# Attention, expert routing and MLP on one core: a build-time estimate that also counts DMA queues, and another order of the first list's vector steps

## The chip, the cores and the metric

The kernel runs on one core of a Trainium2 chip. Its time is the device time of one execution in microseconds (us). Engines are named as the profile names them: PE is TensorE (PEld its weight load), DVE VectorE, ACT ScalarE, POOL GpSimd, SP SyncE, which here only issues transfers.

## The reference, cut to what matters

```python
def reference(**kwargs):
    attn_out = _attn_ref(q, k, v)                    # (2, 8, 768, 64): local window plus block summaries
    x = attn_out.transpose(0, 2, 1, 3).reshape(1536, 512)
    x = _moe_ref(x, w_gate, w1, w2)
    return _moe2_ref(x, w_in, w_out)

def _moe_ref(x, w_gate, w1, w2):                     # 8 experts, 192 tokens each
    logits = x @ w_gate
    for idx in np.argsort(-logits.flatten()):        # greedy: best pair first, until each expert is full
        tok, e = idx // 8, idx % 8
        if assigned[tok] < 0 and counts[e] < 192:
            assigned[tok] = e; counts[e] += 1
    for e in range(8):
        mask = assigned == e
        out[mask] = np.maximum(x[mask] @ w1[e], 0) @ w2[e]

def _moe2_ref(x, w_in, w_out):                       # 512 -> 2048 -> 512
    r = np.maximum(x @ w_in, 0)
    return (r * r) @ w_out
```

## The kernel before, in words

The program has three stretches. Up to about 95 us attention runs, with its projections onto the expert logits. Up to about 318 us routing and experts run side by side: routing finds, one expert after the other, the list of the 192 tokens of the expert that fills up next, and an expert whose list is there is computed while the next lists are found. Then comes the last MLP, `_moe2_ref`, in 48 steps.

**Routing** (function `routing`). For each list DVE compares keys (L566), PE counts (L578), and from the counts come the expert and its threshold. Then DVE picks the tokens, PE sums over them (L786, L787), DVE scans (L790) and turns the positions into two small one-hot arrays (function `t_hot`, L846 to L852). PE multiplies these (`t_idx`, L860), DVE spreads the product (`t_spread`, L869), PE sums (`t_sum`, L878), and POOL gathers the rows of x by the indices (`t_gather`, L904 and L906), into `xa` and `xb`. Between the scan and `t_hot` stand four DVE steps that belong to the next list: `ua` (L802), `cap` (L796), the update of the logits (L797) and `kt` (L820). For the first list they stand behind `t_hot`, for the others ahead of it.

**Experts** (functions `x_t`, `expert`). `x_t` transposes the gathered rows on PE (the row transposes, L942 and L944). An expert has 32 matmuls with w1 (L961) into four tiles, which ACT brings into `ht` (L966), and 32 with w2 (L978) into two tiles, which ACT and DVE split into `yhi` (L984) and `ylo` (L985). The weights of an expert are four tiles, loaded by SP (`w_load`, L931, two transfers of 512 KB each).

**Conversions** (function `conv_stream`). The last MLP multiplies in a form that needs each fp32 weight as a high and a low part. The 4 MB of w_in and 4 MB of w_out are cut into 32 pieces of 512 KB, eight for each quarter of the hidden units. Piece i is loaded by SP into a buffer `raw` (L621), of which there are two. DVE then makes four steps: the first (L636) and second (L640) on piece i, the low part of piece i-1 (L643), and the third step on piece i (L646); ACT makes the high part (L639). The third step is the last reader of the buffer, so piece i+2 can only be loaded behind the third step of piece i:

```python
            nc.vector.scalar_tensor_tensor(fi, raw[:, :, 1], -0x40000000, fi, op0=OP.bitwise_and, op1=OP.bitwise_or)
            nfree[0] = i + 3
            if not eager[0] and i + 2 < len(todo):
                conv_load(i + 2)
```

**What sets the order.** Each engine runs its instructions in the order in which the program was written, and that order is made when the program is built. The class `Clock` (variable `T`) keeps an estimated time for PE, DVE, ACT and POOL; each piece of code adds its estimated cost. The main loop of `moe` takes, whenever the estimated PE is free, the next piece of routing, of row transposes or of an expert, whichever the estimate says can start first. `t_gather` notes when the gathered rows are thought to be there (`d["tx"]`), and `conv_idle` puts conversion steps where the estimate has DVE idle, if the piece is thought to be loaded (`landed`):

```python
        while nload[0] < min(nfree[0], len(todo)) and freed[nload[0]] <= T.pe:
            landed[nload[0]] = T.pe + 5.0
            conv_load(nload[0])
```

**The last MLP.** Step i multiplies by w_in (`hmm`, L1070, 12 matmuls), ACT applies ReLU (L1073), DVE squares (L1074), ACT makes the high part (L1078), DVE the low part (L1079). The square and the low part of one step are called a pair below. Two steps later the result is multiplied by w_out (`omm`, L1096, 12 matmuls). Between two pairs stand six conversion steps in the first 12 steps, until all 32 pieces are converted, with more where a quarter's weights have to be complete (ahead of steps 4, 8 and 12).

Of the kernel before, what the change touches and what calls it, by code (L numbers as in the profile page):

```python
# [9 lines left out]
F32 = mybir.dt.float32  # L10
# [6 lines left out]
OP = mybir.AluOpType  # L17
# [4 lines left out]
N, DM, E, F, FF = 1536, 512, 8, 1024, 2048  # L22
CAP = N // E
NB = S // 32
NBLK = N // 128
# [389 lines left out]
BIG = 2.0 ** 120  # L415
# [4 lines left out]
class Clock:  # L420


    def __init__(self):
        self.pe = self.dve = self.act = self.pool = 0.0

    def p(self, us, after=0.0):
        self.pe = max(self.pe, after) + us
# [164 lines left out]
def moe(tc, nc, R0, x_dram, m_dram, L9, w1, w2, win, wout, out, identf, identb, dbg=None):  # L592
# [19 lines left out]
    nload, nfree, eager = [0], [2], [True]  # L612
# [51 lines left out]
    rp = R0.rp  # L664
    sctx = ExitStack()
    p_s = sctx.enter_context(tc.tile_pool(name="m_ps", bufs=1, space=PSUM, reuse_waits="tile"))
    wt9, low, ones, dead, zero24 = R0.wt9, R0.low, R0.ones, R0.dead, R0.zero24
# [5 lines left out]
    T = Clock()  # L673
# [11 lines left out]
    def routing():  # L685
        tm_at = T.v(0.1)
        for ph in range(E):
            d = st[ph] = {}
            ei = rp.tile([128, 8], U32, name="ei", bufs=4)
            es = rp.tile([128, 1], F32, name="es")  # L690
# [14 lines left out]
            m, mw, o, no = R0.m, R0.mw, R0.o, R0.no  # L705
# [38 lines left out]
            if ph < E - 1:  # L744
                tm = R0.tm
                yield tm_at + 0.1
                ps = p_s.tile([128, 128], F32, name="ms", bufs=3)
# [7 lines left out]
                th = m8[:, 0:1]  # L755
                nc.vector.tensor_scalar(es, ei[:, 0:1], -1.0, 15.0, op0=OP.mult, op1=OP.add)
                T.v(0.9, T.pe + 0.25)
            else:
# [5 lines left out]
                ps = p_s.tile([128, 128], F32, name="ms", bufs=3)  # L764
# [20 lines left out]
            ps = p_s.tile([128, 48], F32, name="ms", bufs=3)  # L785
# [2 lines left out]
            T.p(0.07, sel_at + 0.1)  # L788
            sc = rp.tile([128, 24], F32, name="sc")
            nc.vector.tensor_tensor_scan(sc, ps[:, 24:48], zero24, 0.0, op0=OP.add, op1=OP.add)  # L790
            a = rp.tile([128, NBLK], F32, name="ua")
            cap = rp.tile([128, E], F32, name="cap")

            def full():
                if ph < E - 1:
                    nc.vector.tensor_scalar(cap, wt9[:, 0, 0:E], es, -2 * BIG, op0=OP.is_equal, op1=OP.mult)  # L796
                    nc.vector.tensor_tensor(L9[:, :, 0:E], L9[:, :, 0:E],  # L797
                                            cap[:, None, :].to_broadcast([128, NBLK, E]), op=OP.add)

            def over_th():  # L800
                if ph < E - 1:
                    nc.vector.tensor_scalar(a, m, th, None, op0=OP.is_gt)  # L802

            first = ph == 0
            if not first:
                over_th()
            nc.vector.tensor_tensor(sc, ps[:, 0:24], sc, op=OP.add)
            nc.vector.scalar_tensor_tensor(sc, sc, 1.0, s2, op0=OP.add, op1=OP.mult)
            if not first:
                full()  # L810
            s = d["s"] = rp.tile([128, NBLK], I32, name="s")
            nc.vector.tensor_tensor(s, sc[:, 0:NBLK], sc[:, NBLK:], op=OP.add)
            now = ph < 2 or ph >= E - 2
            if first:
                t_hot(ph)
                over_th()
                full()
            if ph < E - 1:
                kt = rp.tile([128, NBLK], F32, name="kt")
                nc.vector.scalar_tensor_tensor(kt, sc[:, NBLK:], CAP + 0.5, sel[:, 1], op0=OP.is_lt, op1=OP.mult)  # L820
            T.v(1.1, T.pe + 0.2)
            if now and not first:
                t_hot(ph)
            if ph < E - 1:
                nc.vector.tensor_tensor(a, a, kt, op=OP.max)
# [73 lines left out]
    def t_gather(ph):  # L899

        d = st[ph]
        xa = d["xa"] = f1.tile([128, DM], F32, name="xa")
        xb = d["xb"] = f1.tile([128, DM], F32, name="xb")[0:64, :]
        nc.gpsimd.indirect_dma_start(out=xa, out_offset=None, in_=x_dram,  # L904
                                     in_offset=bass.IndirectOffsetOnAxis(ap=sci[:, d["ka"]:d["ka"] + 1], axis=0))
        nc.gpsimd.indirect_dma_start(out=xb, out_offset=None, in_=x_dram,  # L906
                                     in_offset=bass.IndirectOffsetOnAxis(ap=d["ib"][:, :1], axis=0))
        fl = d["fl"] = rp.tile([1, 1], I32, name="fl", bufs=4)
        nc.gpsimd.memset(fl, 0)
        d["tx"] = T.g(2.3, max(d["ix_at"], T.pe) + 0.1) + 2.8  # L910
        w_next()

    wl, done, used = [(ph, i) for ph in range(E) for i in range(4)], [-1], [8]
# [6 lines left out]
    def w_load(ph, i):  # L920

        d = st[ph]
        eng = nc.sync
        if i == 1:
            eng.value_load(d["fl"][0:1, 0:1], min_val=0, max_val=N - 1)
        r = eng.value_load(d["ei"][0:1, 0:1], min_val=0, max_val=E - 1)
        s1 = w1[bass.ds(r, 1)].rearrange("o (k p) f -> p (o k) f", p=128)
        s2 = w2[bass.ds(r, 1)].rearrange("o (k p) f -> p (o k) f", p=128)
        t = wp.tile([128, 4, 512], F32, name="w8")
        for k in (0, 2):  # L930
            eng.dma_start(t[:, k:k + 2, :], s1[:, k:k + 2, 512 * i:512 * i + 512] if i < 2 else  # L931
                          s2[:, 4 * i - 8 + k:4 * i - 6 + k, :])
        d.setdefault("w", []).append(t)

    def x_t(ph):

# [59 lines left out]
    freed, landed = {}, {}  # L996

    def conv_idle():

        while nload[0] < min(nfree[0], len(todo)) and freed[nload[0]] <= T.pe:  # L1000
            landed[nload[0]] = T.pe + 5.0
            conv_load(nload[0])
        while (R is None or len(st) >= done[0] + 4) and T.dve < T.pe - 0.3 and landed.get(nfree[0] - 2, 1e9) <= T.pe:
            n0, f0 = nstep[0], nfree[0]
            conv_step()
            if nstep[0] == n0:
                return
            T.v(0.7, T.pe - 0.7)
            if nfree[0] > f0:
                freed[nfree[0] - 1] = T.dve + 1.0  # L1010
# [162 lines left out]
```

## Time and profile before

| | us |
|---|---|
| three runs | 584.87, 585.63, 586.07 (median 585.63) |
| the profiled execution, its own time | 588.34 |
| its span in the profile | 586.1 |
| PE busy | 566.9 (97%) |
| DVE busy | 344.7 (59%) |
| ACT busy | 196.5 (34%) |
| POOL busy | 82.4 (14%) |
| granted PE clock, mean | 0.997 |

The profiled execution is 2.24 us longer than its span and 2.71 us longer than the median. A busy share is a mean over three stretches with different limits: in the last MLP alone DVE is busy about 85% of the time as long as conversions run, and under 30% afterwards.

### The profile page before, as it was taken

What the parts mean: (1) busy time and instruction counts of PE and PEld (TensorE: products, weight loads), DVE (VectorE), ACT (ScalarE), POOL (GpSimd) and SP (SyncE); (2) the same over time, 40 slices, a digit from 0 to 9 for tenths busy, and PEclk for the clock granted to TensorE, in tenths of its full rate; (3) what the DMA queues carried; (4) which work ended last, traced back from release to release, by engine and by line L of the source; (5) the groups of instructions that cost most, each with busy time, mean ns of one, the idle gap of its engine ahead of it and who ended that gap; (6) DMA issues with size and microseconds to landing.
All of it is one profiled execution on the core that took longest, in us unless ns stands there. A gap on an engine that the chain in (4) does not pass through costs nothing.

```text
span 586.1 us, 10517 instructions
## 1 busy us (share of the span) xinstructions
PE 566.9 (97%) x4128; PEld 474.9 (81%) x4128; DVE 344.7 (59%) x773; ACT 196.5 (34%) x421; POOL 82.4 (14%) x136
## 2 busy tenths in 40 slices
PE   6999997999999999999899999999999999999996
PEld 4777873698888978999899888878888888888884
DVE  6875788877878879655464888872322222222222
ACT  4877861331322314122122333342222122222221
POOL 7663300110401222010000000000300000300002
PEclk9999999999999999999899999999999999999999
DMA  9997114635285374688542354420100000100001
GB/s 228 264 181 161 65 74 144 241 127 193 97 287 172 144 233 155 243 285 308 215 143 74 110 174 126 130 72 2 72 1 1 1 0 1 72 1 0 1 0 72
DMA packets 55392, 71.33 MB, mean 122 GB/s; under 512 B 21296, under 2 KB 32560, under 8 KB 55344
## 3 DMA queue, kind: packets, MB, share of 16 engines
q1 hardware_dynamic: 53360, 64.38, 35.4%
q0 software_dynamic: 1984, 6.29, 3.1%
q8 instruction: 32, 0.52, 0.4%
q14 instruction: 16, 0.13, 0.1%
HBM read 64.37 MB, written 6.29 MB: 121 GB/s over the span
## 4 chain that ended last, share of the span: by engine, by line
PE 61%; issue 15%; DVE 12%; DMA 7%; ACT 2%; POOL 2%; SPq 0%; POOLq 0%; DVEq 0%; ACTq 0%
PE ph L961 12%; PE ph L978 12%; PE pg L1070 9%; PE ph L1096 7%; PE px L1096 2%; PE O L284 2%; PE cnt L578 2%; DMA raw<-in_moe_w_out_dram 2%; DVE f L646 2%; PE S L250 2%; PE T L270 2%; DVE f L640 2%; DMA raw<-in_moe_w_in_dram 2%; DVE G L566 2%; PE T L193 2%
## 5 line engine op out<-in xcount | busy, mean ns | idle before, releaser
L978 PE MATMUL ph<-ht,w 128*128 128x192 f32 x512 | 91.4, 334 | 2.6 <-ACT ht L966 2.6
L961 PE MATMUL ph<-xt,w 128*128 128x192 f32 x512 | 90.9, 331 | 0.0
L566 DVE TENSOR_SCALAR G<-mrow,m 128x1536 bf16<-128x1536 f32 (+4 forms) x108 | 85.0, 839 | 8.1 <-PE cnt L578 5.2
L978 PEld LDWEIGHTS ph<-ht,w 128*128 128x128 f32 x512 | 84.4, 193 | 6.3 <-ACT ht L966 3.2
L961 PEld LDWEIGHTS ph<-xt,w 128*128 128x128 f32 x512 | 82.5, 190 | 3.2 <-issue 2.3
L1070 PE MATMUL pg<-yhi,w 128*128 128x512 f32 x192 | 59.1, 389 | 0.0
L1074 DVE TENSOR_TENSOR xa<-xa 128x512 f32<-128x512 f32 x24 | 16.6, 691 | 56.3 <-ACT xa L1073 56.3
L1109 POOL DMA_INDIRECT out_dram<-f,sci x6 | 5.9, 979 | 308.2 <-DVE f L1107 307.5
L1074 DVE TENSOR_TENSOR xb<-xb 128x512 f32<-128x512 f32 x24 | 16.6, 692 | 53.6 <-ACT xb L1073 53.3
L1070 PEld LDWEIGHTS pg<-yhi,w 128*128 128x128 f32 x192 | 36.0, 188 | 7.5
L1070 PE MATMUL pg<-ylo,w 128*128 128x512 f32 x96 | 37.3, 389 | 0.0
L1096 PE MATMUL ph<-w,xt 128*128 128x512 f32 x144 | 35.7, 391 | 0.2 <-DVE xt L1079 0.2
L966 ACT ACTIVATE ht<-ph 128x384 f32<-128x384 f32 x32 | 15.7, 490 | 55.2 <-PE ph L961 52.9
L1073 ACT ACTIVATE xa<-pg 128x512 f32<-128x512 f32 x24 | 14.3, 594 | 57.9 <-PE pg L1070 57.9
L1073 ACT ACTIVATE xb<-pg 128x512 f32<-128x512 f32 x24 | 14.3, 594 | 54.6 <-PE pg L1070 54.6
L1096 PEld LDWEIGHTS ph<-w,xt 128*128 128x128 f32 x144 | 26.9, 188 | 6.3 <-DVE xt L1079 0.5
L1070 PE MATMUL pg<-yhi,w2a 128*128 128x512 f32 x96 | 29.7, 391 | 0.0
L1070 PE MATMUL pg<-yhi,w2b 128*128 128x512 f32 x96 | 29.5, 389 | 0.0
L263 ACT ACTIVATE P<-S,nm 128x120 f32<-128x120 f32 x96 | 26.6, 371 | 1.8 <-DVE nm L259 1.8
L984 ACT ACTIVATE yhi<-ph 128x384 fp32r<-128x384 f32 x16 | 7.8, 490 | 56.9 <-PE ph L978 56.9
L636 DVE TENSOR_SCALAR f<-raw 128x512 int32<-128x512 int32 x32 | 13.7, 427 | 19.2 <-DMA raw<-in_moe_w_in_dram 12.3
L904 POOL DMA_INDIRECT xa<-x_dram,sci x8 | 13.4, 1669 | 69.2 <-DVE sci L892 43.5
(242 smaller groups left out, 985.6 us busy)
## 6 DMA issues: line engine op xcount, KB each, us to landing
w<-in_moe_w_dram SPq DMA_DIRECT2D x64, 512.0 KB, 6.2
raw<-in_moe_w_in_dram SPq DMA_DIRECT2D x16, 512.0 KB, 3.8
raw<-in_moe_w_out_dram SPq DMA_DIRECT2D x16, 512.0 KB, 3.3
vw<-in_v_dram SPq DMA_DIRECT2D x16, 240.0 KB, 6.3
rawk<-in_k_dram SPq DMA_DIRECT2D x8, 384.0 KB, 6.4
rawq<-in_q_dram SPq DMA_DIRECT2D x8, 384.0 KB, 6.0
x_dram<-x SPq DMA_DIRECT2D x10, 256.0 KB, 2.3
vw<-in_v_dram SPq DMA_DIRECT2D x8, 80.0 KB, 4.9
```

The costliest lines, as they stand in the source:

```text
L193: nc.tensor.transpose(pr[:, r, :], ROWS[nm, b, hp][:, 3 * half + r, :], identf)
L263: nc.scalar.activation(P[u][:, hh, i], SS[u][hh][:, i], AF.Exp, bias=NM[u][:, hh, i:i + 1])
L566: self.nc.vector.tensor_scalar(t[:, used:used + w], self.mrow[:, 128 * j0:128 * j1], self.m[:, c:c + 1], CS, op0=OP.is_le, op1=OP.mult)
L636: nc.vector.tensor_scalar(fi, raw[:, :, 1], 3, 0x3FFFFFF8, op0=OP.logical_shift_left, op1=OP.bitwise_and)
L904: nc.gpsimd.indirect_dma_start(out=xa, out_offset=None, in_=x_dram, in_offset=bass.IndirectOffsetOnAxis(ap=sci[:, d["ka"]:d["ka"] + 1], ax ...
L961: nc.tensor.matmul(ps[:, j, 0:CAP], w[:, k, 128 * (f % 4):128 * (f % 4) + 128], d["xt"][:, k, :], start=(k == 0), stop=(k == 3), skip_grou ...
L966: nc.scalar.activation(d["ht"][:, f0:f0 + 2, :], ps[:, :, 0:CAP], AF.Relu)
L978: nc.tensor.matmul(ps[:, j, 0:CAP], w[:, f % 4, 128 * dd:128 * dd + 128], d["ht"][:, f, :], start=(f == 0), stop=(f == 7), skip_group_chec ...
L1070: nc.tensor.matmul(ps, a[:, k, fs], b[:, k, js], start=(n == 0), stop=(n == 11))
L1073: nc.scalar.activation(r, ps, AF.Relu)
L1074: nc.vector.tensor_tensor(r, r, r, op=OP.mult)
L1096: nc.tensor.matmul(PO[j][t], a[:, 128 * t:128 * t + 128], b[:, f % 4, :], start=(f == 0 and n == 0), stop=(f == 15 and n == 2))
```

## The change

`Clock` gets a fifth time, for the DMA queues (method `d`). Each weight tile adds 3.1 us to it, each gather 1.0 us, each conversion load 1.6 us. The gathered rows are taken to be there between 0.2 and 1.7 us later than before, by how far the DMA time is ahead. A loaded piece is taken to be there 4.4 us behind the later of PE and DMA time, where it was 5.0 us behind PE. In `routing` the first list gets the order of the other lists. No instruction's operands change, and no piece of work is added or removed but three filler matmuls (35 where there were 32).

```diff
     def __init__(self):
-        self.pe = self.dve = self.act = self.pool = 0.0
+        self.pe = self.dve = self.act = self.pool = self.dma = 0.0
+
+    def d(self, us, after=0.0):
+        self.dma = max(self.dma, after) + us
+        return self.dma
...
-            a = rp.tile([128, NBLK], F32, name="ua")
-            cap = rp.tile([128, E], F32, name="cap")
-
-            def full():
-                if ph < E - 1:
-                    nc.vector.tensor_scalar(cap, wt9[:, 0, 0:E], es, -2 * BIG, op0=OP.is_equal, op1=OP.mult)
-                    nc.vector.tensor_tensor(L9[:, :, 0:E], L9[:, :, 0:E],
-                                            cap[:, None, :].to_broadcast([128, NBLK, E]), op=OP.add)
...
-            first = ph == 0
-            if not first:
-                over_th()
+            if ph < E - 1:
+                a = rp.tile([128, NBLK], F32, name="ua")
+                nc.vector.tensor_scalar(a, m, th, None, op0=OP.is_gt)
             nc.vector.tensor_tensor(sc, ps[:, 0:24], sc, op=OP.add)
+            if ph < E - 1:
+
+                cap = rp.tile([128, E], F32, name="cap")
+                nc.vector.tensor_scalar(cap, wt9[:, 0, 0:E], es, -2 * BIG, op0=OP.is_equal, op1=OP.mult)
             nc.vector.scalar_tensor_tensor(sc, sc, 1.0, s2, op0=OP.add, op1=OP.mult)
-            if not first:
-                full()
+            if ph < E - 1:
+                nc.vector.tensor_tensor(L9[:, :, 0:E], L9[:, :, 0:E], cap[:, None, :].to_broadcast([128, NBLK, E]),
+                                        op=OP.add)
...
-            now = ph < 2 or ph >= E - 2
-            if first:
-                t_hot(ph)
-                over_th()
-                full()
...
-            if now and not first:
+            now = ph < 2 or ph >= E - 2
+            if now:
                 t_hot(ph)
...
-        d["tx"] = T.g(2.3, max(d["ix_at"], T.pe) + 0.1) + 2.8
+        out = T.g(2.3, max(d["ix_at"], T.pe) + 0.1)
+        d["tx"] = out + 3.0 + 0.5 * min(max(T.dma - out, 0.0), 3.0)
+        T.d(1.0, out)
...
         d.setdefault("w", []).append(t)
+        T.d(3.1, T.pe)
...
-            landed[nload[0]] = T.pe + 5.0
+            landed[nload[0]] = T.d(1.6, T.pe) + 2.8
             conv_load(nload[0])
```

Lines move with it. In the order after the change L621 is L625, the DVE steps L636, L640, L643, L646 are L640, L644, L647, L650, ACT's L639 is L643, L966 is L961, L984 is L979, L948 is L943, L931 is L925, L1074 is L1069 and L1079 is L1074.

**ACT, the seventh expert (number 6).** From its row transposes (`xt`) to its second `yhi`; the rows with `f` as input are the conversions' high parts. Before:

```order
L948 ACTIVATE xt<-px 128x2x192
L948 ACTIVATE xt<-ms 128x2x192
L639 ACTIVATE w2a<-f 128x512
L966 ACTIVATE ht<-ph 128x384 x2
L639 ACTIVATE w2a<-f 128x512
L966 ACTIVATE ht<-ph 128x384
L639 ACTIVATE w2a<-f 128x512
L966 ACTIVATE ht<-ph 128x384
L639 ACTIVATE w2a<-f 128x512
L984 ACTIVATE yhi<-ph 128x2x192
L639 ACTIVATE w2a<-f 128x512
```

After the change:

```order
L943 ACTIVATE xt<-px 128x2x192
L943 ACTIVATE xt<-ms 128x2x192
L643 ACTIVATE w2a<-f 128x512
L961 ACTIVATE ht<-ph 128x384 x3
L643 ACTIVATE w2a<-f 128x512
L961 ACTIVATE ht<-ph 128x384
L643 ACTIVATE w2a<-f 128x512
L979 ACTIVATE yhi<-ph 128x2x192
L643 ACTIVATE w2a<-f 128x512
```

(The two rows ahead of these are the row transposes of the last expert, number 7.) Ahead of the expert's fourth `ht` there stood the high parts of pieces 3, 4 and 5; now there stand those of pieces 2 and 3.

**DVE, the last MLP from the second pair to the third.** Rows with `raw` alone as input are first steps, those with `raw,f` second (L640 before, L644 after) and third steps (L646 before, L650 after), those with `f,w2b` low parts. Before:

```order
L1074 TENSOR_TENSOR xa<-xa 128x512
L1079 TENSOR_TENSOR xt<-xa,xt 128x512
L636 TENSOR_SCALAR f<-raw 128x512
L640 SCALAR_TENSOR_TENSOR f<-raw,f 128x512
L643 TENSOR_TENSOR w2b<-f,w2b 128x512
L646 SCALAR_TENSOR_TENSOR f<-raw,f 128x512
L636 TENSOR_SCALAR f<-raw 128x512
L640 SCALAR_TENSOR_TENSOR f<-raw,f 128x512
L1074 TENSOR_TENSOR xb<-xb 128x512
```

After the change:

```order
L1069 TENSOR_TENSOR xa<-xa 128x512
L1074 TENSOR_TENSOR xt<-xa,xt 128x512
L650 SCALAR_TENSOR_TENSOR f<-raw,f 128x512
L640 TENSOR_SCALAR f<-raw 128x512
L644 SCALAR_TENSOR_TENSOR f<-raw,f 128x512
L647 TENSOR_TENSOR w2b<-f,w2b 128x512
L650 SCALAR_TENSOR_TENSOR f<-raw,f 128x512
L640 TENSOR_SCALAR f<-raw 128x512
L1069 TENSOR_TENSOR xb<-xb 128x512
```

The pairs now fall at other places in the round of four conversion steps: this one ahead of a third step, the next behind a first step, where before they fell behind a third and behind a second step. Of the conversion steps, 53 stood ahead of the first pair, and 48 do now.

**SP, from the load of piece 2 on.** The `w_` rows are the second weight tile of expert 7, in two halves. Before:

```order
L621 DMA raw<-in_moe_w_in_dram 128x1024
L925 TENSOR_LOAD fl
L925 ISA x2
L926 TENSOR_LOAD ei
L926 ISA x2
L931 ISA
L931 DMA w_4110<-in_moe_w_dram 128x2x512
L931 ISA
L931 DMA w_4110<-in_moe_w_dram 128x2x512
L621 DMA raw<-in_moe_w_in_dram 128x1024
L621 DMA raw<-in_moe_w_out_dram 128x1024
```

After the change:

```order
L625 DMA raw<-in_moe_w_in_dram 128x1024 x2
L919 TENSOR_LOAD fl
L919 ISA x2
L920 TENSOR_LOAD ei
L920 ISA x2
L925 ISA
L925 DMA w_4114<-in_moe_w_dram 128x2x512
L925 ISA
L925 DMA w_4114<-in_moe_w_dram 128x2x512
```

Piece 3 now stands ahead of this tile. The third and fourth tile of expert 7 follow in both orders; piece 4 stood ahead of them and now stands behind them.

## Rows read from the trace of the kernel before

**Rows 1.** Waits of PE from 95 us on: us in total, times, longest us.
```profile
PE ph L978 <- ACT ht L966: 2.6, 1, 2.6
PE px L942 <- DMA xa<-x_dram,sci: 1.2, 1, 1.2
PE px L944 <- DMA xb<-x_dram,ib: 0.9, 1, 0.9
```

**Rows 2.** Timeline near 287 us, DVE, ACT, PE: start, us, instruction, [idle before <- releaser].
```profile
272.79 0.43 DVE L636 TENSOR_SCALAR f<-raw 128x512 int32<-128x512 int32 x1 [0.97 <-DMA raw<-in_moe_w_in_dram]
...
283.60 0.43 DVE L636 TENSOR_SCALAR f<-raw 128x512 int32<-128x512 int32 x1 [5.72 <-DMA raw<-in_moe_w_out_dram]
...
286.00 0.63 ACT L639 ACTIVATE w2a<-f 128x512 fp32r<-128x512 f32 x1 [5.58 <-DVE f L646]
...
287.06 10.40 PE L978 MATMUL ph<-ht,w 128*128 128x192 f32 x52 [2.62 <-ACT ht L966]
```

**Rows 3.** Chain that ended last, the next 64 matmul records: start us, us, what.
```profile
297.46 10.40 PE ph L961 x64
```

**Rows 4.** Stretch by engine: PE, PEld, DVE, ACT, POOL busy, granted PE clock, DMA.
```profile
290.00:292.00 2.00, 2.00 (x8) 2.00 (x8) 0.96 (x2) 0.00 (x0) 0.00 (x0) 0.52 0.42 168
```

**Rows 5.** Timeline of DVE, last MLP: the second pair to the third, and pair 12.
```profile
327.14 0.68 DVE L1074 TENSOR_TENSOR xa<-xa 128x512 f32<-128x512 f32 x1
328.52 0.69 DVE L1079 TENSOR_TENSOR xt<-xa,xt 128x512 fp32r<-128x512 f32 x1 [0.70 <-ACT xt L1078]
329.13 0.42 DVE L636 TENSOR_SCALAR f<-raw 128x512 int32<-128x512 int32 x1
...
330.80 0.68 DVE L646 SCALAR_TENSOR_TENSOR f<-raw,f 128x512 int32<-128x512 int32 x1
331.40 0.42 DVE L636 TENSOR_SCALAR f<-raw 128x512 int32<-128x512 int32 x1
331.85 0.69 DVE L640 SCALAR_TENSOR_TENSOR f<-raw,f 128x512 int32<-128x512 int32 x1
332.67 0.69 DVE L1074 TENSOR_TENSOR xb<-xb 128x512 f32<-128x512 f32 x1
...
391.52 0.69 DVE L1079 TENSOR_TENSOR xt<-xb,xt 128x512 fp32r<-128x512 f32 x1 [0.70 <-ACT xt L1078]
```

**Rows 6.** Timeline of PE at the w_out matmuls of step 12.
```profile
391.56 0.48 PE L1096 MATMUL ph<-w,xt 128*128 128x512 f32 x1
392.27 2.14 PE L1096 MATMUL ph<-w,xt 128*128 128x512 f32 x8 [0.23 <-DVE xt L1079]
```

**Rows 7.** Third steps, the loads behind them on SP, the first steps that wait for these.
```profile
301.80 0.68 DVE L646 SCALAR_TENSOR_TENSOR f<-raw,f 128x512 int32<-128x512 int32 x1
302.51 0.33 SPq L621 DMA_DIRECT2D raw<-in_moe_w_in_dram  x1
306.29 0.43 DVE L636 TENSOR_SCALAR f<-raw 128x512 int32<-128x512 int32 x1 [1.26 <-DMA raw<-in_moe_w_in_dram]
...
371.26 0.33 SPq L621 DMA_DIRECT2D raw<-in_moe_w_out_dram  x1
375.68 0.43 DVE L636 TENSOR_SCALAR f<-raw 128x512 int32<-128x512 int32 x1 [0.18 <-DMA raw<-in_moe_w_out_dram]
```

**Rows 8.** The 32 loads of L621, from issue to landing.
```profile
DMA to landing us min/median/max: 3.1/3.7/11.2
```

**Rows 9.** Timeline of DVE: scan (L790) and spread (L869) of lists 0 and 1.
```profile
97.18 0.21 DVE L790 TENSOR_TENSOR_SCAN sc<-ms,zero 128x24 f32<-128x24 f32 x1 [0.29 <-PE ms L787]
100.64 0.36 DVE L869 TENSOR_TENSOR hs<-diag,ms 128x208 f16<-128x208 f16 x1
...
120.15 0.21 DVE L790 TENSOR_TENSOR_SCAN sc<-ms,zero 128x24 f32<-128x24 f32 x1 [0.46 <-PE ms L787]
123.38 0.37 DVE L869 TENSOR_TENSOR hs<-diag,ms 128x208 f16<-128x208 f16 x1
```

More of the change, by code (lines that the diff above doesn't have):

```diff
@@ L790, in routing @@
             nc.vector.tensor_tensor_scan(sc, ps[:, 24:48], zero24, 0.0, op0=OP.add, op1=OP.add)
-            a = rp.tile([128, NBLK], F32, name="ua")
-            cap = rp.tile([128, E], F32, name="cap")
-            def full():
-                if ph < E - 1:
-                    nc.vector.tensor_scalar(cap, wt9[:, 0, 0:E], es, -2 * BIG, op0=OP.is_equal, op1=OP.mult)
-                    nc.vector.tensor_tensor(L9[:, :, 0:E], L9[:, :, 0:E],
-                                            cap[:, None, :].to_broadcast([128, NBLK, E]), op=OP.add)
-            def over_th():
-                if ph < E - 1:
-                    nc.vector.tensor_scalar(a, m, th, None, op0=OP.is_gt)
-            first = ph == 0
-            if not first:
-                over_th()
+            if ph < E - 1:
+                a = rp.tile([128, NBLK], F32, name="ua")
+                nc.vector.tensor_scalar(a, m, th, None, op0=OP.is_gt)
             nc.vector.tensor_tensor(sc, ps[:, 0:24], sc, op=OP.add)
+            if ph < E - 1:
+                cap = rp.tile([128, E], F32, name="cap")
+                nc.vector.tensor_scalar(cap, wt9[:, 0, 0:E], es, -2 * BIG, op0=OP.is_equal, op1=OP.mult)
             nc.vector.scalar_tensor_tensor(sc, sc, 1.0, s2, op0=OP.add, op1=OP.mult)
-            if not first:
-                full()
+            if ph < E - 1:
+                nc.vector.tensor_tensor(L9[:, :, 0:E], L9[:, :, 0:E], cap[:, None, :].to_broadcast([128, NBLK, E]),
+                                        op=OP.add)
             s = d["s"] = rp.tile([128, NBLK], I32, name="s")
             nc.vector.tensor_tensor(s, sc[:, 0:NBLK], sc[:, NBLK:], op=OP.add)
-            now = ph < 2 or ph >= E - 2
-            if first:
-                t_hot(ph)
-                over_th()
-                full()
             if ph < E - 1:
```

## The prediction

> **What bounds the kernel now.** I read the waits of PE first, then the timelines around them. PE is busy 97% of the span, so a change can only win where PE stands still or runs at a lower clock, and lose where it makes PE wait. Behind the attention PE waits in three places of any size [rows 1]: 2.6 us for an `ht` of ACT, 1.2 and 0.9 us for gathered rows.
>
> The longest wait is a convoy. The reader is to see it step by step in [rows 2]. DVE sits 5.72 us until piece 5 of the weights has landed, at 283.60. Its third step ends about 286.0, then ACT makes the high part of piece 5 (0.63 us), and only behind that, in ACT's order, stands the fourth `ht` of expert 6, for which PE has waited 2.62 us. The wait also costs clock. PE goes on at 287.06 and needs 10.40 us for 52 matmul records, where the next 64 records take the same 10.40 us [rows 3]. At that pace 52 would take 8.45, so 1.95 us went to the lower of the two clock levels: a granted clock of 0.52, that is 1.2 GHz instead of 2.4, stands in the stretch from 290 to 292 us [rows 4]. The place costs 2.62 + 1.95 = 4.57 us.
>
> The second thing to see is that in the first part of the last MLP DVE is as full as PE, with nothing to spare. From the second pair to the third pass 332.67 - 327.14 = 5.53 us [rows 5], with no idle in them but the 0.70 us for ACT's high part and 0.2 us ahead of the square. PE, which takes its results two steps later, starts with a lead in hand, and by step 12 DVE has used it up: pair 12 gives its low part at 391.52, PE wants it at 391.56 and waits 0.23 us [rows 5, 6]. From there every us more that DVE needs before pair 12 is a us of the kernel.
>
> **The change part by part.** *The convoy.* In ACT's order the fourth `ht` of expert 6 now stands behind the high parts of pieces 2 and 3 instead of 3, 4 and 5. Piece 3 was in the buffer at 272.79 even behind a weight tile that now comes after it [rows 2]; its four DVE steps (2.27 us [rows 5]) and a high part of 0.63 us are done before 277, 7 us before PE wants that `ht`, at 287.06 - 2.62 = 284.44. Piece 5 now stands behind the first `yhi`. Piece 4 is issued later, behind two more weight tiles, but the same transfers were all in at 283.60; its steps and its high part end about 286.5, and the `yhi` that stands behind them is wanted 20 records of 0.1625 us after 284.44, at 287.7. So I take the wait and its clock loss away: **-4.6 us**. Bounds: -2.6 if the clock still falls, -4.6 if both go. What is late next is the start of the last MLP, which begins that much earlier, as do its conversions.
>
> *The gathers.* The estimate of the row transposes is later, but PE's order has them at the same place in seven of eight lists, and one matmul later in list 1. The waits of 1.2 and 0.9 us are those of lists 2 and 4 and stay: **0**. The cover that moved conversions would need in the routing stays too, for no conversion but two single steps is in it.
>
> *The first list.* From scan to spread DVE needs 100.64 - 97.18 = 3.46 us in list 0 and 123.38 - 120.15 = 3.23 us in list 1, which already has the order that list 0 gets [rows 9]. The one-hot arrays of list 0 come later, but the spread behind them waits for the same seven steps in both orders, so its indices come up to 0.23 us earlier. Against that stands one filler matmul and one expert matmul moved by a place on PE, some 0.2 us. I take **0**, bounds -0.3 and +0.3.
>
> *Five conversion steps more in the full stretch.* 48 instead of 53 conversion steps stand ahead of the first pair, where DVE had idle time, so five more stand between there and pair 12. A round of four steps takes 331.40 - 329.13 = 2.27 us, so five take 2.8. Against it: before every second pair DVE idles 0.21 us, seen as 0.82 us between the last second step and the square [rows 5] where a step takes some 0.6 otherwise, for the ReLU waits on ACT behind a high part. In the new order that high part is a step or two earlier, and six such gaps (1.3 us) go. **+1.5 us**, bounds 1.5 and 2.8.
>
> *The refill of the two buffers.* This is the term that decides. Piece i+2 is issued 0.71 us after the start of the third step of piece i, and its first step could start 3.78 us behind that in one case, 4.42 in another [rows 7]; the quickest landing of all was 3.1 us [rows 8]. So from third step to the first step two pieces on at least 3.8 us are needed, more often 4.5 (0.71 + 3.78). What stands between is the third step itself, then first, second, low part and third step of the next piece: 0.60 + 2.27 = 2.87 us. If a pair stands among these, it adds 329.13 - 327.14 = 1.99 us [rows 5], together 4.86: enough, or short by 0.2. A pair comes every six steps. In the order before it always stood behind a third or a second step, and then each refill has one. In the new order every other pair stands just ahead of a third step, and the next one behind the first step two pieces on: that refill has none. I count seven of them up to pair 12 (pieces 15, 18, 21, 24, 26, 29, 31). Before, the wait of 1.26 us at 306.29 [rows 7] is such a refill with none, and the nearest row in kind. By its 4.49 us, each costs 4.49 - 2.87 = 1.62 us: 7 x 1.62 = **+11.3 us**. Bounds: with 3.1 us, 0.94 each, 6.6; with 4.42, 2.26 each, 15.8. The trace has this wait for "DMA raw" only as 0.18 us in the whole stretch now, since the pair covers it.
>
> The Trainium skill ("DMA: Bandwidth & Descriptors", section "Anatomy of one DMA — SWDGE (gpsimd) path") gives for that path a fit of 2.0 us plus bytes over 436 GB/s, an estimate of 3.2 us for 512 KB. By it a refill would be short by 1.04 us, seven by 7.3, and the kernel 4.0 us quicker than by my sum; no load of these rows was that quick to be used, and the 3.78 us of [rows 7] decides.
>
> *The clock behind it.* PE gets these delays as waits: its lead covers the first, the last is the longest, before the w_out matmuls of step 12, for ahead of that pair 12 conversion steps stand in a row (9 before) with one of the seven refills among them. A wait of some 4 us is nearest to the one of 2.62, which was followed by a clock loss of 1.95 us, so I add **+1.9 us** for the one wait behind which nothing waits for DVE any more; bounds 0 and 1.9. Losses behind the earlier waits only shorten the next wait.
>
> **Sum:** -4.6 + 0 + 0 + 1.5 + 11.3 + 1.9 = **+10.1 us**. From the profiled execution's own 588.34 this gives 598.4; from the median of 585.63, which is 2.71 lower, **595.7**. Bounds: low -4.6 - 0.3 + 1.5 + 6.6 + 0 = +3.2, 588.8; high -2.6 + 0.3 + 2.8 + 15.8 + 1.9 = +18.2, 603.8.
>
> **The rivals.** *The refills are in time.* If loads came within 2.2 us, or PE's lead covered DVE, only the convoy and the five steps count: -4.6 + 1.5 = -3.1, 582.5, faster. It decides at a refill under 2.87 us from third step to first. Against: the quickest landing of 3.1 us [rows 8], and the 0.23 us at step 12 [rows 6], which leaves no lead. For: this late hardly any other transfer runs. Chance 0.08.
>
> *It cancels.* With waits of about 0.4 us each, 2.8 in all, the loss meets the gain: within 0.2% (1.2 us, about what a measurement of this kernel can tell from no change), 585.6. Chance 0.03.
>
> *The convoy only moves.* Piece 4 lands late behind the two weight tiles and holds `yhi`, and PE waits at expert 7 instead. For: piece 5, behind these tiles, came late [rows 2], and the margin worked out above is 1.2 us. Against: PE needs the buffer that this `yhi` frees only two tiles later. Then the -4.6 is gone: +14.7, 600.3. Chance 0.08.
>
> *The clock stays low.* PE's waits come every second step, and in [rows 4] the level is 1.2 GHz behind one wait. If it stayed there for the five steps 8 to 12, each would take twice its 5.5 us, 27.5 us more, of which the waits worked out above for these steps, some 9 us, are filled: +18 on top of the sum without its 1.9, 612. Against it: behind the one long wait the loss was 1.95 us and over by 297 [rows 2, 3]. Chance 0.03. The Trainium skill ("TensorE: Matmul & The Clock Gate", section "Part 1: The HAM clock gate") has it that the throttled level is the default and that activity releases it; with PE's activity broken every second step that speaks for this rival.
>
> **How the numbers follow.** The forecast has 0.78, 595.7. Faster by over 0.2% is the first rival, 0.08; within 0.2% the second, 0.03; slower the rest, 0.89. The range leaves out the first, second and fourth rival (0.14) and the outermost ends of the forecast, and takes in the third: 590 to 601.
>
> **What would show it.** The wait of PE for `ht` L966 is gone and expert 6's 64 w2 records take 10.4 us. DVE's waits for "DMA raw" ahead of first steps in the last MLP rise from 0.2 to about 11 us in seven places, PE waits for `xt` and `ht` low parts every second step up to step 12, and from there on PE has no wait. The forecast is wrong if those seven waits are missing or under 0.5 us each, or if the low part of pair 12 comes less than 70 us after the square of the second pair (391.52 - 327.14 = 64.4 us now, 77 by the terms above).

## The result, and the profile after

The changed kernel takes **592.98 us** (median of 592.71, 592.95, 593.0 and 595.4), the kernel before 585.85 in the same comparison. The ratio is 1.0121, with a 95% interval of 1.0073 to 1.0168: slower, by 7.1 us in the medians. The profiled execution after took 592.71 us, close to its median. That of before (588.34) was 2.7 us above its own median, so the two traces differ by only 4.4 us.

The head of the page after, busy times as shares of the span:

```profile
span 590.5 us, 10523 instructions
PE 570.6 (97%) x4131; PEld 475.8 (81%) x4131; DVE 342.6 (58%) x773; ACT 195.9 (33%) x421; POOL 81.2 (14%) x136
```

No share has moved by more than a point. The time shows in what the engines wait for. First DVE's groups by line in the last MLP, 318 to 396 us: busy time, mean ns of one, then the idle time ahead of them and what ended it. The first row is from before, the second from after.

```profile
L636 DVE TENSOR_SCALAR f<-raw 128x512 int32<-128x512 int32 x18 | 7.6, 422 | 0.2 <-DMA raw<-in_moe_w_out_dram 0.2
L640 DVE TENSOR_SCALAR f<-raw 128x512 int32<-128x512 int32 x19 | 8.1, 424 | 8.4 <-DMA raw<-in_moe_w_in_dram 4.5 <-DMA raw<-in_moe_w_out_dram 3.8
```

The first conversion steps waited 8.4 us for loads, where before it was 0.2. Those 8.4 us lie in seven places, and the loads behind all seven are in the chain that ended last (issue us, us until landed, what):

```profile
324.17 3.02 DMA raw<-in_moe_w_out_dram
335.80 3.74 DMA raw<-in_moe_w_in_dram
348.15 3.22 DMA raw<-in_moe_w_out_dram
359.98 3.62 DMA raw<-in_moe_w_in_dram
368.06 3.60 DMA raw<-in_moe_w_in_dram
380.27 3.08 DMA raw<-in_moe_w_out_dram
387.69 3.11 DMA raw<-in_moe_w_out_dram
```

One of the seven in DVE's timeline (start us, us, instruction, idle time before it and its releaser), from the second pair to the third:

```profile
321.47 0.68 DVE L1069 TENSOR_TENSOR xa<-xa 128x512 f32<-128x512 f32 x1
322.85 0.69 DVE L1074 TENSOR_TENSOR xt<-xa,xt 128x512 fp32r<-128x512 f32 x1 [0.70 <-ACT xt L1073]
323.46 0.69 DVE L650 SCALAR_TENSOR_TENSOR f<-raw,f 128x512 int32<-128x512 int32 x1
324.06 0.42 DVE L640 TENSOR_SCALAR f<-raw 128x512 int32<-128x512 int32 x1
324.52 0.69 DVE L644 SCALAR_TENSOR_TENSOR f<-raw,f 128x512 int32<-128x512 int32 x1
325.13 0.69 DVE L647 TENSOR_TENSOR w2b<-f,w2b 128x512 fp32r<-128x512 f32 x1
325.73 0.68 DVE L650 SCALAR_TENSOR_TENSOR f<-raw,f 128x512 int32<-128x512 int32 x1
327.29 0.43 DVE L640 TENSOR_SCALAR f<-raw 128x512 int32<-128x512 int32 x1 [0.88 <-DMA raw<-in_moe_w_out_dram]
327.63 0.69 DVE L1069 TENSOR_TENSOR xb<-xb 128x512 f32<-128x512 f32 x1
...
394.56 0.68 DVE L1069 TENSOR_TENSOR xb<-xb 128x512 f32<-128x512 f32 x1
395.94 0.69 DVE L1074 TENSOR_TENSOR xt<-xb,xt 128x512 fp32r<-128x512 f32 x1 [0.70 <-ACT xt L1073]
```

The pair stands just ahead of the third step at 323.46, the next pair just behind the first step at 327.29. Between these two steps there is no pair, only four conversion steps, and DVE stands still for 0.88 us. [Rows 5] have the same stretch without such an idle. The last two rows are pair 12. Its low part comes 395.94 - 321.47 = 74.47 us after the square of the second pair, where before it was 64.38: 10.1 us more.

PE's waits from 95 us to the end (us in total, times, longest) answer to [rows 1]:

```profile
PE ph L1091 <- ACT ht L1073: 1.8, 1, 1.8
PE pg L1065 <- ACT w L643: 1.6, 1, 1.6
PE px L939 <- DMA xb<-x_dram,ib: 1.0, 1, 1.0
PE ph L1091 <- ACT xt L1073: 0.9, 1, 0.9
```

The 2.6 us for an `ht` of ACT are gone, and one of the two waits for gathered rows. The same view of before has one more row, the second longest, which [rows 1] leave out:

```profile
PE ms L860 <- DVE hot L852: 1.5, 1, 1.5
```

There PE waited for the one-hot arrays of list 0. This wait is gone too, but PE runs filler matmuls in its place, and the matmuls behind it come no earlier: 2.17 us behind the scan of list 0, 2.08 before. What the list saved is counted below.

Three waits of any size in the last MLP have come. PE's timeline at expert 6 and at step 12:

```profile
281.19 10.56 PE L973 MATMUL ph<-ht,w 128*128 128x192 f32 x64
291.60 8.61 PE L956 MATMUL ph<-xt,w 128*128 128x192 f32 x52
...
395.96 0.50 PE L1091 MATMUL ph<-w,xt 128*128 128x512 f32 x1 [0.92 <-ACT xt L1073]
396.69 2.10 PE L1091 MATMUL ph<-w,xt 128*128 128x512 f32 x8 [0.23 <-DVE xt L1074]
```

Expert 6 does its 64 w2 records in one piece, 10.4 us to the next start. The convoy of [rows 2] cost 4.57 us there.

**Where the time went.** Four marks cut both traces: the scan of list 0, the first w_in matmul of the last MLP, the first w_out matmul of step 12, the end.

| stretch, us | before | after | difference |
|---|---|---|---|
| start to scan of list 0 | 97.18 | 97.88 | +0.70 |
| to the first w_in matmul (317.96, 312.26) | 220.78 | 214.38 | -6.40 |
| to the w_out matmuls of step 12 (391.56, 395.96) | 73.60 | 83.70 | +10.10 |
| to the end of the span | 194.54 | 194.54 | 0 |

The second line is the convoy (-4.55), one gather wait less (-1.1) and list 0 (-0.7, below). The third is what the seven waits (8.35 in their sum) and five conversion steps more cost; the 1.75 of the steps is what is left, not a reading of its own. Behind step 12 nothing is left of either.

### The profile page after: what moved, and what is told of

It reads as the page before. It is cut to its first block, busy times and chain, and to the rows that moved or that the text cites. A ratio compares the mean times of both kernels' runs of the same rounds, so it can differ in the third digit from the quotient of the medians.

```text
span 590.5 us, 10523 instructions
## 1 busy us (share of the span) xinstructions
PE 570.6 (97%) x4131; PEld 475.8 (81%) x4131; DVE 342.6 (58%) x773; ACT 195.9 (33%) x421; POOL 81.2 (14%) x136
## 3 DMA queue, kind: packets, MB, share of 16 engines
q1 hardware_dynamic: 53360, 64.38, 34.7%
## 4 chain that ended last, share of the span: by engine, by line
PE 65%; issue 14%; DVE 10%; DMA 6%; ACT 2%; POOL 2%; SPq 0%; POOLq 0%; DVEq 0%; ACTq 0%
PE ph L956 15%; PE ph L973 14%; PE pg L1065 9%; PE ph L1091 7%; PE px L1091 2%; PE cnt L582 2%; PE O L284 2%; DMA raw<-in_moe_w_out_dram 2%; PE S L250 2%; PE T L270 2%; DMA raw<-in_moe_w_in_dram 2%; DVE G L570 2%; PE T L193 1%; DVE f L650 1%; DMA rawq<-in_q_dram 1%
## 5 line engine op out<-in xcount | busy, mean ns | idle before, releaser
L973 PE MATMUL ph<-ht,w 128*128 128x192 f32 x512 | 89.3, 329 | 0.0
L973 PEld LDWEIGHTS ph<-ht,w 128*128 128x128 f32 x512 | 82.9, 190 | 3.1 <-issue 2.9
L1069 DVE TENSOR_TENSOR xa<-xa 128x512 f32<-128x512 f32 x24 | 16.6, 690 | 56.0 <-ACT xa L1068 56.0
L1069 DVE TENSOR_TENSOR xb<-xb 128x512 f32<-128x512 f32 x24 | 16.6, 690 | 53.6 <-ACT xb L1068 53.6
L961 ACT ACTIVATE ht<-ph 128x384 f32<-128x384 f32 x32 | 15.7, 491 | 60.2 <-PE ph L956 57.9
L979 ACT ACTIVATE yhi<-ph 128x384 fp32r<-128x384 f32 x16 | 7.8, 490 | 63.1 <-PE ph L973 63.1
L640 DVE TENSOR_SCALAR f<-raw 128x512 int32<-128x512 int32 x32 | 13.6, 424 | 16.4 <-DMA raw<-in_moe_w_out_dram 9.4
L644 DVE SCALAR_TENSOR_TENSOR f<-raw,f 128x512 int32<-128x512 int32 x32 | 22.1, 690 | 0.8
```

Of the source, the lines that this page charges most:

```text
L640: nc.vector.tensor_scalar(fi, raw[:, :, 1], 3, 0x3FFFFFF8, op0=OP.logical_shift_left, op1=OP.bitwise_and)
L644: nc.vector.scalar_tensor_tensor(fi, raw[:, :, 0], 29, fi, op0=OP.logical_shift_right, op1=OP.bitwise_or)
L961: nc.scalar.activation(d["ht"][:, f0:f0 + 2, :], ps[:, :, 0:CAP], AF.Relu)
L973: nc.tensor.matmul(ps[:, j, 0:CAP], w[:, f % 4, 128 * dd:128 * dd + 128], d["ht"][:, f, :], start=(f == 0), stop=(f == 7), skip_group_chec ...
L1069: nc.vector.tensor_tensor(r, r, r, op=OP.mult)
```

## The experiments

The theory: seven refills of the two `raw` buffers lost the pair that had covered them, because the pairs fall at other places among the conversion steps. The rivals: the mere number of steps done early, or the list, or the row of steps ahead of step 12. The direct test, a third `raw` buffer, was not made. The runs move the pairs instead. Below, "w_in to step 12" is the third line of the table above. The kernel before was timed again in each of the three series (medians 585.6, 586.28, 586.93), so kernels of different series are compared by their ratios.

**Shifting the pairs by a few steps.** The first four runs put n conversion steps ahead of the last MLP's loop, three in the changed kernel and one in the kernel before:

```diff
+    conv_step(n)
     for i in range(len(seq) + LAG):
```

n = 1:

> The changed kernel with one conversion step more ahead of the last MLP's first step (49 instead of 48). Of the seven refills without a pair three are left (pieces 26, 29, 31). Theory (a refill without a pair costs DVE about 1.2 us, and PE's lead is used up): four waits of 0.9 to 1.6 us go, 5.0 us in all, and one step of 0.57 us leaves the full stretch: 592.98 - 5.6 = 587.4. Rival (what counts is only how many steps stand ahead of the first pair): 592.98 - 0.6 = 592.4. Rival (the waits come from transfers that the new order moved): all seven waits stay, 592.4.

n = 2:

> The changed kernel with two conversion steps more ahead of the first step (50). Seven refills have no pair again (pieces 14, 17, 20, 23, 26, 29, 31), so two steps more do less than one. Theory: seven waits of about 1.2 us stay, two steps of 0.57 us leave the full stretch: 592.98 - 1.1 = 591.9, some 4.5 us slower than with one step more. Rival (number of steps): 591.9 as well, but then faster than with one step more (592.4).

n = 5:

> The changed kernel with five conversion steps more ahead of the first step (53, as many as before the change, and no refill without a pair). Theory: the last MLP runs as before the change, and what the change wins ahead of it (5.7 us to the first matmul of the last MLP) stays: 585.85 - 5 = 581, no later than 583; DVE's waits for DMA raw between the pairs under 0.5 us in all. Rival (number of steps): 592.98 - 2.8 = 590.1. Rival (moved transfers): the waits stay, 590.

n = 1 in the kernel **before**:

> The kernel before with one conversion step more ahead of the last MLP's first step (54 instead of 53): six refills lose their pair (pieces 15, 18, 21, 24, 27, 30). Nothing else changes, the wait at expert 6 stays. Theory: six waits of about 1.2 us come, less one step of 0.57: 585.85 + 6.6 = 592.5. Rival (number of steps, or moved transfers): same or 0.6 us faster, 585.3.

With n = 3 and n = 7 in the changed kernel, in the second series:

> The changed kernel with three conversion steps more ahead of the first step of the last MLP: 51, and one refill without a pair (piece 31) instead of seven. Theory (alignment): six of the seven waits go, 6 x 1.2 = 7.2, and three steps of 0.57 us (1.7) leave the full stretch: 593.0 - 8.9 = 584.1 if all of it was on the path, 1 us more where PE bounds instead; 583.5 to 585.5. Rival (the time follows the number of steps ahead: 49 gave 589.0, 50 gave 592.5, 53 gave 583.9): about 588 to 590, or on a line between its neighbours.

> The changed kernel with seven conversion steps more: 55, no refill without a pair. Theory: with 53 steps and no such refill PE already bounds the stretch (its waits there come to 0.8 us in all), so two steps fewer bring between 0 and 0.8 us over the 583.9 of five steps: 583.1 to 584.2. Rival (the number of steps ahead counts by itself, 0.57 us each): 582.8 or less. If DVE came late for the first pair because of the seven steps in a row, PE would wait at the first w_out matmuls and the time would rise above 584.5.

| kernel | steps ahead | refills without a pair | waits for raw, us | w_in to step 12 | ratio to before (95%) |
|---|---|---|---|---|---|
| before | 53 | 0 | 0.2 | 73.60 | 1 |
| before, n = 1 | 54 | 6 | 7.6 | 79.21 | 1.012 (1.009 to 1.015) |
| after | 48 | 7 | 8.35 | 83.70 | 1.0121 (1.0073 to 1.0168) |
| after, n = 1 | 49 | 3 | 3.7 | 78.85 | 1.0077 (1.0048 to 1.0107) |
| after, n = 2 | 50 | 7 | 8.4 | 82.39 | 1.0139 (1.0107 to 1.017) |
| after, n = 3 | 51 | 1 | 1.5 | 76.23 | 0.9999 (0.9976 to 1.0022) |
| after, n = 5 | 53 | 0 | 0.8 | 74.86 | 0.9963 (0.9941 to 0.9984) |
| after, n = 7 | 55 | 0 | 0.6 | 74.63 | 0.9978 (0.9957 to 0.9999) |

The time does not follow the number of steps alone: n = 2 is slower than n = 1, and in the kernel before one step more, which by its number should only help, costs 6.6 us. It follows mainly the refills without a pair, which the order gives. The number of steps counts beside them: the kernel before with n = 1 has twice the waits of n = 1 in the changed one (7.6 and 3.7 us), but five steps more ahead, and both need about the same from w_in to step 12. Five steps in front take the whole loss away and leave part of what was won ahead of the last MLP: 583.93 us against 585.6.

n = 2 and the kernel before with n = 1 came within 0.7 us of the theory's numbers, n = 1 1.6 us above. n = 5 missed its bound of 583 by 0.9 us: its stretch up to step 12 took 1.26 us more than before, and the 5.7 us won ahead of the last MLP were read from two profiled executions, not from medians. n = 7 took 584.87, above the 584.5 from which I had looked for PE waiting at the first w_out matmuls; its trace has no wait there, and PE's waits of 0.8 us stand at step 12. n = 3 was expected at 583.5 to 585.5 and took 586.42. In its profiled execution (586.4) the excess stands at step 12:

```profile
388.03 0.51 PE L1091 MATMUL ph<-w,xt 128*128 128x512 f32 x1 [1.84 <-ACT xt L1073]
388.75 3.25 PE L1091 MATMUL ph<-w,xt 128*128 128x512 f32 x8 [0.22 <-DVE xt L1074]
```

and, by engine, with the granted PE clock as the third number from the end:

```profile
390.00:392.00 2.00, 2.00 (x6) 1.52 (x6) 1.30 (x3) 1.08 (x2) 0.00 (x0) 0.50 0.00 0
```

The one refill left falls late, so PE takes it as a single wait of 1.84 us. Behind it the clock fell to 0.50, 1.2 GHz, and from step 12 to the end the kernel needed 196.17 us where all others of the table needed 194.5: 1.6 us that I had not counted. That is shown for this execution only; other executions of n = 3 took 584.5 to 588.7 us.

**The two parts of the change apart.** The new order of the first list alone, in the kernel before:

```diff
-            if first:
-                t_hot(ph)
-                over_th()
-                full()
...
+            if now:
+                t_hot(ph)
```

> The kernel before with only the first list's new order; the estimate is the old one. Conversions stand as before: 53 steps ahead of the first pair, no refill without a pair. Theory: the scan to spread of list 0 falls from 3.46 to about 2.8 us, which is all the edit brings; PE's wait of 2.6 us for the fourth ht of expert 6 stays, and the seven waits do not appear. Kernel before minus 0.7 us: 585.0, between 584.5 and 586. Rival (the first list's order is a cause of the loss): at least 1 us slower than before, over 587.

It took 586.46 us, above the expected 584.5 to 586, but the kernel before took 586.28 in this series; ratio 0.9991 (0.997 to 1.0012): nothing that can be measured. In its trace the scan of list 0 starts at 96.58 and the spread at 99.35, 2.77 us where [rows 9] have 3.46, as in the changed kernel. So the edit does shorten that chain by 0.7 us, and this is lost in the scatter. No wait for raw is over 0.2 us in the last MLP, and the convoy is there:

```profile
284.81 8.72 PE L966 MATMUL ph<-ht,w 128*128 128x192 f32 x52 [2.13 <-ACT ht L954]
```

The estimate alone, in the changed kernel with the first list's old order (the reverse of that diff):

> The changed kernel with the first list's old order: the new estimate alone, 48 conversion steps ahead of the first pair and seven refills without a pair between. Theory: the ht wait of expert 6 is gone, the seven waits are there (0.9 to 1.6 us each), and list 0 needs 3.46 us again: 0.7 us above the changed kernel, 593.7, between 592.5 and 595. Rival (part of the loss is the first list's): near or below 591.

594.71 us, ratio 1.014 (1.0111 to 1.0169): the whole loss, with seven waits of 1.0 to 1.5 us (8.4 in all) and 83.75 us from w_in to step 12. Both convoy and refills are the estimate's doing.

**Where else the steps can stand.** The same five steps, but behind the first pair:

```diff
-        conv_step(SF if i < 16 else 1)
+        conv_step((SF + 5 if i == 0 else SF) if i < 16 else 1)
```

> The changed kernel, 48 conversion steps ahead of the first pair as in it, but 11 instead of 6 steps between the first pair and the second. From the second pair on the pairs stand as with five steps more ahead; one refill without a pair is left (piece 14), early, where PE has its lead. Theory (where the pairs stand among the conversion steps decides): six of the seven waits go and the time is that of five steps more ahead (ratio to before 0.9963), up to 1.2 us more: 583.5 to 585.5. Rival (the number of steps ahead of the last MLP decides): as the changed kernel, 591 to 593.5.

587.68 us, ratio 1.0014 (0.9989 to 1.0039): not the 592 of the rival, but 2 to 4 us above the theory's numbers. From w_in to step 12 it needs 77.86 us, 3.0 more than with the five steps in front (74.86). Its early refill costs 1.21 us; I had taken that as covered by PE's lead, and DVE has no such reserve. The remaining 1.8 us are the five steps themselves: in front they fill the time in which DVE waits for the first ReLU (2.28 us ahead of the first square here, none with five steps in front), behind the first pair they stand in the full stretch.

The last three move w_out. Ahead of step 12 stands a row of conversions, because a quarter's w_out is made complete together with its w_in, though it is used two steps later:

```diff
-            while ndone[0] < min(len(todo), 8 * (i // 4) + 8):
+            while ndone[0] < min(len(todo), 8 * (i // 4) + 4):
                 conv_step()
             hmm(i)
         if i >= LAG:
+            while ndone[0] < min(len(todo), 8 * ((i - LAG) // 4) + 8):
+                conv_step()
```

> The changed kernel, but a quarter of w_out has to be complete only ahead of the w_out matmuls that use it (two steps later than now), not ahead of the w_in matmuls of the same quarter. 48 steps ahead of the first pair; of 80 conversion steps between the first pair and pair 12 (of step 12) 72 are left, and six refills without a pair. Theory: six waits of 1.2 us (7.2) instead of 8.35, and eight steps of 0.57 us (4.6) fewer on the path to pair 12: 593.0 - 1.2 - 4.6 = 587.2, and a wait for the low part of step 12 or 14 is still there; 586 to 589. Rival (the row of conversions ahead of step 12 causes the loss, the refills do not): all of the wait goes, 584 or less.

With `SF - 1` at i = 0 in the line of the diff before:

> As the one before, and between the first pair and the second five conversion steps instead of six: one step less, and no refill without a pair. Theory: no wait for raw over 0.5 us, PE waits for nothing from the first to the twelfth step, which then take 73.6 to 74.2 us from the first w_in matmul to the first w_out matmul of step 12 (73.60 before, 83.70 in the changed kernel); 582 to 584. Rival (DVE needs its steps early, however they stand): slower than with six steps, over 587.

With `conv_step(5)` ahead of the loop:

> w_out later as in the two before, with five conversion steps more ahead of the first step of the last MLP; no refill without a pair. Theory: the 0.4 to 0.7 us of PE waits at step 12 that five steps more had left go as well; PE alone bounds the stretch: 73.6 us from the first w_in matmul to the w_out matmuls of step 12 (74.86 with five steps more alone): 582.5 to 583.7, the quickest of the kernels with q3. Rival (PE was the bound already): as five steps more, 583.9.

They took 591.07 (ratio 1.0067, 1.0032 to 1.0102), 588.96 (1.0036, 1.0014 to 1.0057) and 582.71 us (**0.9929**, 0.9905 to 0.9953). The first came out as neither theory nor rival. The second is over the rival's 587, but quicker than with six steps, where the rival had it slower; the theory's 582 to 584 failed. The first shows that the row ahead of step 12 was not the cause: with it gone, six refill waits remain (8.1 us) and the kernel is still slower than before; PE's wait has only moved to the w_in matmuls of step 12 (2.8 us for an ACT high part). In the second no wait for raw is over 0.4 us, and yet it is slower than before. Its PE timeline:

```profile
373.19 0.50 PE L1065 MATMUL pg<-yhi,w 128*128 128x512 f32 x1 [0.54 <-DVE w L647]
374.45 0.50 PE L1065 MATMUL pg<-yhi,w 128*128 128x512 f32 x1 [0.53 <-ACT w L643]
377.66 0.80 PE L1065 MATMUL pg<-yhi,w 128*128 128x512 f32 x1 [2.70 <-DVE w L647]
378.68 4.04 PE L1091 MATMUL ph<-w,xt 128*128 128x512 f32 x9
```

I had looked only at what w_out's pieces hold up. But the w_in matmuls of step 12 want the last w_in piece two steps before its w_out matmuls, and in this order its low part stands behind pair 11 (DVE, at 376.92). PE waits 2.70 us for it and then runs nine matmuls in 4.04 us instead of 2.20 (as in the last of these runs), at a granted clock of 0.50 from 376 to 382 us. Here the number of steps done early does decide, through the place of one low part. With five steps in front that low part stands a pair earlier, and all that PE waits for from 300 us to the end of that kernel is this:

```profile
PE pg L1065 <- DVE w L647: 0.2, 1, 0.2
```

From w_in to step 12 it needs 74.09 us. It is the quickest version: 0.7% below the kernel before, about 2% below the changed one.

## Why the prediction was right, point by point

The forecast was slower, 595.7 us in a range of 590 to 601; 592.98 was measured. The mechanism was the one forecast, with the seven pieces named; three sizes were off. The number came nearer than its terms, and that is partly luck: the sum was made from the trace, where +10.1 us stands against a measured +4.4, and was then added to a median that lies 2.7 us below the traced execution (from that execution's own time it gives 598.4, against 592.71).

- **The convoy, -4.6: right.** 64 records without a wait in 10.4 us, 4.55 us less in the traces. In another run the convoy was cheaper: with the list alone 2.13 us of wait and no lower clock (52 records in 8.72 us, granted 1.00). If some executions of the kernel before are like that, it is part of why its profiled execution was above its median, and why the medians lie further apart (7.1) than the traces (4.4); that is not shown. The rival by which the convoy only moves is out: expert 7 has no wait.
- **The gathers, 0: right for the change, but the rows scatter.** One of the two waits was missing in the profiled execution after; see the last section.
- **The first list, 0: mis-sized.** Its chain got 0.7 us shorter, more than twice the bound I gave (0.3). I counted the same instructions at the same durations in both orders and took list 1 for the new one. What the new order saves is time between instructions that need each other's result (last section).
- **Five steps more, +1.5: near, with luck in the parts.** 10.1 us more up to pair 12, less 8.35 of refill waits, leaves 1.75; the five steps behind the first pair gave 1.8. But I took six idle gaps of 0.21 us ahead of squares to go, 1.3 us, from one that I had read. The trace before has them as 0.21, 0.21, 0.13, 0.07 and 0.01, 0.6 in all. The rest came from what I had not counted: small waits of DVE that went (0.5), and squares that start 0.34 us behind a first step, where a second step starts 0.46 behind it (0.6 in five places).
- **Seven refills, +11.3: right in count, too large by 2.4 to 3 us.** The step that failed is "by its 4.49 us": I gave all seven the price of the one refill at 306.29 [rows 7], which loads a piece of w_in, while four of the seven load w_out. In the chain above the three w_in loads landed 3.60 to 3.74 us after issue, the four w_out loads 3.02 to 3.22. Counted as I did, from third step to first step less 2.87, a w_in refill cost 1.59 us, near my 1.62, and a w_out refill 1.05: 8.9 in all. (DVE's idle time of 8.35 is a little less, for the last step itself runs 0.08 us longer than to the usual next start.) The fit of the Trainium skill ("DMA: Bandwidth & Descriptors", section "Anatomy of one DMA — SWDGE (gpsimd) path") gave an estimate of 3.2 us a load and 7.3 us for the seven. The trace stands at 3.34 on average and 8.35, nearer to it than to my sum, though these loads are issued by SP and the fit is for another path.
- **The clock behind the last wait, +1.9: did not come.** I expected waits at every second step and a last one of some 4 us at step 12. PE took the delay mainly in three pieces, from step 8 on, 1.84, 1.58 and 0.92 us, all three behind high parts of ACT, and behind the last one the clock stayed at 1.00. The lower clock came behind the two earlier ones, where it shortened the next wait, as the text had said. With n = 3 and with the estimate alone the last wait was 1.84 and 2.59 us, and there the 1.6 us did come. So the term was real, but it hung on how the waits were shared out.
- **The clock stays low: it did not.** Behind two waits it was 0.52 at 368 to 370 us and 0.50 at 382 to 384. Between them, and from 388 on, it was 1.00.

Both prices of a refill stood in the trace before. One is the w_in load of [rows 7], issued at 302.51 with the queues nearly empty (from 300 to 302 us the DMA share, the number before the last, is 0.02). The other is a w_out refill without a pair, at 289.20, which I did not use:

```profile
300.00:302.00 2.00, 2.00 (x14) 2.00 (x13) 0.81 (x2) 1.01 (x2) 0.00 (x0) 1.00 0.02 8
289.20 0.43 DVE L636 TENSOR_SCALAR f<-raw 128x512 int32<-128x512 int32 x1 [0.98 <-DMA raw<-in_moe_w_out_dram]
```

Three idle times of 1.26 us and four of 0.98 make 7.7, where 8.35 came. The kernel reads a w_in piece as parts of rows and a w_out piece as whole rows; that this is the reason is not shown.

The sum with the measured sizes: -4.55 - 0.7 - 1.1 + 1.75 + 8.35 + 0.70 (the attention ended later) = +4.4 us, the difference of the two traces.

## What to carry to other kernels

Where a buffer ring is refilled by an instruction in a full, in-order queue, list for each refill what stands between the release of the buffer and its next use. A change of the order upstream can take the one filler out of every second such gap without touching the ring. If work has to be shifted, shift it by a whole period of the two patterns, or test several shifts: neighbours differed by up to 1.4% here, some 8 us (n = 2 and n = 3). And price a transfer by rows of its own kind: here loads of the same size from two tensors differed by 0.5 us.

## What the runs showed of the hardware that I had not expected

**DVE's small steps start later when each needs the one before.** The new order of the first list issues the same steps, yet needs 0.7 us less from scan to spread. DVE's timeline in the old order (the estimate alone):

```profile
96.42 0.21 DVE L794 TENSOR_TENSOR_SCAN sc<-ms,zero 128x24 f32<-128x24 f32 x1 [0.29 <-PE ms L791]
96.66 0.18 DVE L811 TENSOR_TENSOR sc<-ms,sc 128x24 f32<-128x24 f32 x1
96.88 0.18 DVE L812 SCALAR_TENSOR_TENSOR sc<-sc,sel 128x24 f32<-128x24 f32 x1
97.09 0.17 DVE L816 TENSOR_TENSOR s<-sc 128x12 int32<-128x12 f32 x1
97.30 0.17 DVE L850 TENSOR_SCALAR lo<-s 128x12 int32<-128x12 int32 x1
```

and in the new one (the changed kernel):

```profile
97.88 0.21 DVE L794 TENSOR_TENSOR_SCAN sc<-ms,zero 128x24 f32<-128x24 f32 x1 [0.29 <-PE ms L791]
98.00 0.21 DVE L797 TENSOR_SCALAR ua<-m,m 128x12 f32<-128x12 f32 x1
98.12 0.18 DVE L798 TENSOR_TENSOR sc<-ms,sc 128x24 f32<-128x24 f32 x1
98.22 0.22 DVE L802 TENSOR_SCALAR cap<-wt,es 128x8 f32<-128x8 f32 x1
98.35 0.18 DVE L803 SCALAR_TENSOR_TENSOR sc<-sc,sel 128x24 f32<-128x24 f32 x1
98.48 0.26 DVE L805 TENSOR_TENSOR L<-L,cap 128x96 f32<-128x96 f32 x1
98.65 0.16 DVE L808 TENSOR_TENSOR s<-sc 128x12 int32<-128x12 f32 x1
```

In the old order each step reads the result of the one before, and the starts lie 0.21 to 0.24 us apart. In the new one a step that reads something else stands between, starts lie 0.10 to 0.17 us apart, and the chain's own steps (L794, L798, L803, L808) still follow each other in 0.24, 0.23 and 0.30 us, against 0.24, 0.22 and 0.21 us without a step between. Such a filler is nearly free. The Trainium skill ("VectorE: DVE Perf Modes", section "The DRAIN you can't avoid") says that the next step does not start until the pipe of the one before is empty. The same section of the Trainium skill adds that a next step which is not held starts earlier. The traces have both: in the old order L811 starts at 96.66, behind the end of L794 at 96.63, and in the new one L797 at 98.00, ahead of the end of L794 at 98.09. The spread follows at 99.88 in the first (3.46 us behind the scan) and at 100.65 in the second (2.77).

**One gather instruction has two durations.** POOL's gathers into `xa` for lists 2 and 4 take either 1.83 or 3.5 us, from run to run and without any change ahead of them. In the changed kernel's trace both stand side by side:

```profile
153.21 3.52 POOL L896 DMA_INDIRECT xa<-x_dram,sci  x1 [4.03 <-DVE ib L880]
...
201.86 1.83 POOL L896 DMA_INDIRECT xa<-x_dram,sci  x1 [4.06 <-DVE ib L880]
```

After the long one PE waited about 1 us for the rows, after the short one it did not. Before, both were long. With n = 1, 2 and 3 list 2 was short and list 4 long, and with one step less and w_out later both were short. That is 1 us a list of scatter that no edit made; what decides it stays open.

**A wait of PE costs clock or not.** Behind waits of 0.92 us (after) and 1.22 us (before, n = 1) at step 12 the clock stayed at 1.00; behind 1.84 and 2.59 us at the same place it fell to 0.50 and cost 1.6 us. At expert 6 a wait of 2.06 us (before, n = 1) was followed by a granted clock of 0.50 from 286 to 288 us and 0.70 in the next 2 us, and one of 2.13 us (the list alone) by none below 1.00. A wait's length alone does not tell it.
